# Step 1's other-half products in a pair of their own, inverse pieces ahead of the first rounds, and placings split around a key's copy: one change to a DeltaNet and PReLU feed-forward kernel

## The chip, the cores and the metric

The kernel runs on one core of one Trainium2 chip. The core has a matrix engine (TensorE, "PE" in the profile; its weight loads are "PEld"), three engines for elementwise work (VectorE "DVE", ScalarE "ACT", GpSimd "POOL"), and SyncE ("SP"), which here only issues DMA transfers. Each engine works through its own queue of instructions in order; an instruction that needs another engine's result waits on a semaphore, and everything behind it in the same queue waits with it. TensorE writes its products to PSUM (eight banks for each partition; this kernel takes them as two single banks and three pairs at the start), the other engines read them there and write to SBUF.

The metric is the device time of one execution in microseconds (us), as the median of several runs.

## The reference, cut to what matters

```python
def _attn_ref(q, k, v, beta):                      # (4, 8, 768, 48): batch, heads, sequence, head size
    k_n = k / (np.linalg.norm(k, axis=-1, keepdims=True) + 1e-06)
    state = np.zeros((B, H, D, D))
    for t in range(S):
        kt, vt, bt = k_n[:, :, t], v[:, :, t], beta[:, :, t, None]
        y[:, :, t] = np.einsum('bhd,bhde->bhe', q[:, :, t], state)
        v_old = np.einsum('bhde,bhd->bhe', state, kt)
        state = state + bt[:, :, :, None] * np.einsum('bhd,bhe->bhde', kt, vt - v_old)

def _moe_ref(x, w_in, w_out, alpha):               # x: (3072, 384), w_in: (384, 2048)
    h = x @ w_in
    g = np.maximum(h, 0.0) + alpha * np.minimum(h, 0.0)
    return g @ w_out

# the attention's y, with its heads side by side, is x of the feed-forward part
```

All of it is in 32-bit floating point. The recurrence over 768 positions is computed in chunks of 64: within a chunk a triangular system is solved, and between chunks the 48x48 state of each head is carried on.

## The kernel before, in words

A *step* n is one chunk of 64 positions of two of the four batch entries, so there are 12 chunks x 2 = 24 steps; steps 0 and 1 are the first chunk, 2 and 3 the second, and so on. For each step the kernel turns the keys on TensorE (`flip`, L430, with a ScalarE copy to `k_t`, L439 or L456), makes their products (`grams`, L502), turns the right-hand side by the inverse of a unit triangular matrix (`solve`, L884, with VectorE's `u` at L888), and makes the outputs (`outputs`, L897) and the next state (`next_state`, L916). Between these, TensorE works on the feed-forward products (L1062 and L1105, L1126 and others), which make up most of its time; they are woven between the steps' parts by an order written out by hand, which the compiler keeps on each engine.

The inverse is made for four steps at once on VectorE: 64 columns are cut in two halves of 32, and `eliminate` works through a 32x32 block by rounds of two instructions (`prod` at L594, `block` at L600). What it makes is turned back in four pieces each (`turns`, L567: `turned` and then `inverse`), and `place` and `placing` copy a step's share to where TensorE reads it: part 0 is `diag<-turned` (L764), parts 1 and 2 the two halves of `inv`, part 3 two small copies of `wgt` (L775).

For the first four steps there is a shorter way, `eliminate_small`: only blocks of 16 are inverted, and the rest is made up by three *rounds* of substitution k = 0, 1, 2 (`substitute`, L727, and the VectorE additions of `substituted`, L734 and L736). For steps 0 and 1 this is done in `first_chunk`, which runs alone, without feed-forward products to fill TensorE's gaps, since their inputs are not there yet. It begins with `off_products` (L686, L688): TensorE multiplies the turned blocks of both steps by `mid`. For heads in the upper half the product is written twice, to the own half of the partitions (`own[i]`, one PSUM pair for each step) and to the other half (`other`, one pair for both steps, one bank each). ScalarE copies the first kind to `diag` (L689), VectorE copies the second kind to `away` (L692; `aways[i]`). Then the rounds go back and forth between TensorE and VectorE, for step 0 and step 1 in turn; behind step 0's products of round 0 TensorE turns key 4, and behind those of round 1 key 5 (both into the pair that held `other`), and ScalarE copies both to `k_t` (L439). VectorE's four `inverse` pieces (`next(inverted)`) are spread between its other work: two ahead of `aways[0]`, one ahead of `aways[1]`, the last behind round 0's first addition. `place_inverse` (L741) scales the pieces to `inv` with two ScalarE instructions for each step.

Steps 2 and 3 are then done together in `second_pair`, with `alongside(products, pieces)` putting a number of feed-forward products and of weight conversions between the parts. Steps 4 and 5 are done by `attention(n)`, steps from 6 (`JOINED`) on by `burst_a`, `turn_round` and `burst_b`, and three stretches in each step take up feed-forward products and elimination rounds; `PIECES_OF` says how many elimination pieces each of a step's three stretches takes.

The tiles' dependences are tracked for a whole tile: who reads one bank of a pair waits for the last write to that pair.

Of the kernel before, what the change touches and what calls it, by code (L numbers as in the profile page):

```python
# [44 lines left out]
def kernel(  # L45
# [623 lines left out]
    def off_products(both):  # L669

        x = [act[:, FP - 4 + i].rearrange("p f i -> p (f i)") for i in both]
        x = [y.rearrange("p (h c) -> p h c", h=H) for y in x]
        for i in both:
            own = turned[0][:, i * H : i * H + H]
            nc.scalar.mul(x[i][:, :, 0:HB], own, which[:, 0:1])
            nc.vector.tensor_scalar_mul(x[i][:, :, HB:C], own, which[:, 1:2])
        n = C - LB
        own, other = [ps_big(), None], ps_big()
        own[1] = ps_big()
        for i in both:  # L680
            p = own[i][:, 0, 0 : H * n].rearrange("p (b i) -> p b i", b=H)
            q = other[:, i, 0 : G * n].rearrange("p (b i) -> p b i", b=G)
            for b in range(H):
                for t in range(2):
                    w, y = x[i][half(t), b], mid[i][half(t), b, LB:C]
                    nc.tensor.matmul(p[half(t), b], w, y)  # L686
                    if b >= G:
                        nc.tensor.matmul(q[half(1 - t), b - G], w, y)  # L688
            nc.scalar.copy(diag[i][:, :, LB:C], p)  # L689
            other_.append(q)  # L690
        return [
            lambda i=i: nc.vector.tensor_copy(out=away[i][:, :, LB:C], in_=other_[i])  # L692
            for i in both
        ]
# [43 lines left out]
    def place_inverse(n):  # L738

        for i in range(2):  # L740
            nc.scalar.mul(  # L741
                inv[n % NE][:, :, HB * i : HB * i + HB], inverse[0][:, n * H : n * H + H],
                which[:, i : i + 1],
            )

    def place(n, parts=(0, 1, 2, 3)):
        for _ in placing(n, parts):
            pass
# [709 lines left out]
    def attention(n):  # L1458

        assert n + EARLY + 1 < TURNED_K  # L1460
        copies = between_1(n + 1)
        made = through_state(n)
        now(made[:3])
        now(copies)
        now(made[3:])
        yield
        now(solve(n))
        made = grams(n + EARLY)
        now(made[:2])
        now(between_2(n + 1))  # L1470
        now(made[2:])
        scale_v(n + 1)
        yield
        now(outputs(n))
        now(next_state(n))
        load_late(n + 2)
        squares(n + EARLY + 1)
        if n == JOINED - 1:
            flips(n + EARLY + 1, n + 2)
        yield  # L1480
        if n < JOINED - 1:
            flips(n + EARLY + 1, n + 2)
        to_ffn(n)
        if n < JOINED - 1:
            place(n + 2, (0,))
        now(weigh(n + EARLY + 1))
        if n == JOINED - 1:
            load_early(TURNED_K)
        load_q(n + 3)
        load_v(n + 3)  # L1490
        yield
# [113 lines left out]
    def first_chunk(mask, inverted, convert):  # L1605

        both = (0, 1)
        ahead[0] = n_in
        aways = off_products(both)
        for i in both:  # L1610
            for _ in range(2 - i):
                next(inverted)
            aways[i]()
        now_at = {}
        for i in both:
            now_at[i] = rhs_[i]
        for k in range(3):
            for i in both:
                p = substitute(i, now_at[i], k)
                if k == 0:  # L1620
                    now_at[i] = work.tile([128, 2, G, D], FP32, name="r")
                substituted(i, now_at[i], p, k)
                if i == 0 and k < 2:
                    now(flipped(NJ + k, ps_one()))
                if (k, i) == (0, 0):
                    next(inverted)
                    assert next(inverted, None) is None
                if (k, i) == (0, 1):
                    for j in both:
                        place_inverse(j)  # L1630
                        place(j, (3,))
                    for j in (3, 2):
                        off_blocks(j, by_pool=True)
                if (k, i) == (1, 1):
                    begin_in(6)
                if i == 0 and k > 0:
                    mask(0, k - 1)
        for i in both:
            squared(NJ + i)
        for i in both:  # L1640
            rhs_[i] = now_at[i]
        weighted = solve(0)
        keys = flipped(NJ + 2, ps_one())
        now(weighted)
        for a in range(2):
            mask(1, a)
        now(keys)
        now(solve(1))
        convert(6)
        for i in both:  # L1650
            now(outputs(i))
        load_early(NJ + NKE)
        fetch_in(n_in + 4)
        for i in both:
            to_ffn(i, ps_ffn())
        norms(NJ)
        ahead[0] = FT * DM
        convert(4)
        norms(NJ + 1)
# [155 lines left out]
    n = 12  # L1815
# [15 lines left out]
    def second_pair():  # L1831

        n, m, x = 2, 3, NJ
        both = (n, m)
        now(next_state(0))
        load_late(2)
        load_v(3)
        alongside(2, 1)
        now(next_state(1))
        for _ in part(convert_on, 2):  # L1840
            pass
        load_late(3, (0,))
        fetch_in(n_in + 6)
        load_late(3, (1,))
        alongside(4, 1)
        off_product(n)
        flips(x + 3, n)
        squares(x + 2)
        now(weigh(x))
        alongside(3, 1)  # L1850
        off_product(m)
        place_inverse(n)
        place(n, (3,))
        flips(N, m)
        alongside(4, 2)
        load_q(n + 3)
        load_early(x + 1 + NKE)
        fetch_out(1)
        for i in both:
            scale_v(i)  # L1860
        now(weigh(x + 1))
        alongside(3, 1)
        y = ps_big()
        pieces, masks, now_at = [], [], {}
        for i in range(2):
            *made, last = through_state(n + i, None, y[:, :, i * G * D : (i + 1) * G * D])
            pieces += made
            masks.append(last)
        now(pieces + masks)
        place_inverse(m)  # L1870
        place(m, (3,))
        load_q(n + 2)
        load_early(x + 2 + NKE)
        now(weigh(x + 2))
        alongside(4, 2)
        for i in both:
            now_at[i] = rhs_[i]
        for k in range(3):
            y = ps_big()
            made = [  # L1880
                substitute(i, now_at[i], k, y[:, :, j * G * D : (j + 1) * G * D])
                for j, i in enumerate(both)
            ]
            for i, p in zip(both, made):
                now_at[i] = by_parity(nv[i])
                substituted(i, now_at[i], p, k)
            if k == 0:
                now(grams(x))
                squares(x + 3)
                fetch_out(2)  # L1890
                load_v(4)
                alongside(6, 4)
            elif k == 1:
                now(grams(x + 1))
                fetch_out(3)
                load_early(x + 3 + NKE)
                now(weigh(x + 3))
                alongside(6, 3)
            else:
                now(grams(x + 2))  # L1900
                alongside(5, 3)
        for i in both:
            rhs_[i] = now_at[i]
        y = ps_big()
        pieces = []
        for i in range(2):
            pieces += solve(n + i, y[:, :, i * G * D : (i + 1) * G * D])
        now(pieces)
        alongside(2, 1)
        now(grams(x + 3))  # L1910
        alongside(3, 1)
        y = ps_big()
        pieces = []
        for i in range(2):
            pieces += outputs(n + i, y[:, :, i * G * D : (i + 1) * G * D])
        now(pieces)
        alongside(4, 1, (part(blocks, PIECES), PIECES))
        for i in both:
            to_ffn(i)
        for i in both:  # L1920
            alongside(2 * (m - i), 0)
            now(next_state(i))
            load_late(i + 2)
            load_v(i + 3)
        alongside(IN_PARTS - 48, 1, (part(blocks, 1), 1))
# [78 lines left out]
    for n in range(NJ, JOINED):  # L2004
# [7 lines left out]
    assert next(late, None) is None  # L2012
    PIECES_OF = {
        JOINED: (3, WHOLE - 2 * PIECES - 6 - 2 * share - 3, 2 * PIECES),
        JOINED + 1: (0, 4, 7), JOINED + 2: (4, 5, 9), JOINED + 3: (1, 1, 4),
    }
    TURNS = [(3, 3, 4), (3, 3, 4), (4, 4, 4), (0, 5, 6)]
    FILL = {JOINED: (8, 12, 12), JOINED + 1: (10, 12, 10), JOINED + 2: (8, 10, 12)}
# [93 lines left out]
```

## Time and profile before

| | us |
|---|---|
| median of 3 runs | 635.11 (634.94 to 636.32) |
| the profiled execution | 635.72 |
| its span, first to last instruction | 634.0 |
| TensorE busy in the span | 619.7 |
| VectorE busy | 503.8 |
| ScalarE busy | 310.4 |
| GpSimd busy | 98.1 |

The span of the profiled execution is 1.7 us shorter than its time, and its time is 0.6 us above the median. All times in what follows are counted from the start of the span. In the timeline, a row gives the start, the length, the engine, the line, what it writes and reads, the shape and how many instructions of that kind were merged; in brackets at its end stands how long the engine was idle before it and what ended that. A 32-bit matmul is recorded twice, so that 16 of the program's products appear as x32. "issue" is idle time for which the profile shows nothing that was waited for.

### The profile page before, as it was taken

Reading aid. Unit: us, or ns where it says so; the run is one execution under the profiler, and the core shown is the slowest. Engines: PE = TensorE matmul, PEld = TensorE weight load, DVE = VectorE, ACT = ScalarE, POOL = GpSimd, SP = SyncE. Lnnn points to the kernel's source line nnn. Section 1 sums busy time; section 2 is a strip of 40 time slices with the busy share of each in tenths; the row PEclk is TensorE's granted clock in tenths of the full one; section 3 lists DMA queues with packets and bytes.
Section 4 is the critical chain, followed back from the end, with each engine's and each line's share of the span. In section 5 each row is a group of like instructions: output and inputs, shape, how many; then the busy total and the mean of one; then the engine's idle time right before and its main releaser. Section 6 shows DMA issues by size and latency. Waiting matters only on the chain.

```text
span 634.0 us, 21642 instructions
## 1 busy us (share of the span) xinstructions
PE 619.7 (98%) x9116; PEld 549.2 (87%) x9116; DVE 503.8 (79%) x1219; ACT 310.4 (49%) x814; POOL 98.1 (15%) x214
## 2 busy tenths in 40 slices
PE   6889999999999999999999999999999999999997
PEld 5568888567789988989989989988999999999997
DVE  5888999979989988958978968878979579486383
ACT  6878466245543245545444546335357356353230
POOL 7021211010000000000000000000053062071350
PEclk9999999999999999999999999999999999999999
DMA  7958835212253241242242121211220300100100
GB/s 122 303 126 183 251 56 170 44 38 44 46 79 54 51 76 28 45 76 36 43 77 35 37 43 27 46 32 27 46 49 12 65 15 9 32 3 1 26 1 25
DMA packets 145968, 39.26 MB, mean 62 GB/s; under 512 B 139040, under 2 KB 142256, under 8 KB 145872
## 3 DMA queue, kind: packets, MB, share of 16 engines
q1 hardware_dynamic: 144000, 37.40, 28.9%
q8 instruction: 71, 1.16, 0.7%
q10 hardware_dynamic: 1872, 0.49, 0.4%
q14 instruction: 25, 0.20, 0.1%
HBM read 33.14 MB, written 4.72 MB: 60 GB/s over the span
## 4 chain that ended last, share of the span: by engine, by line
PE 90%; ACT 3%; DVE 2%; SPq 2%; DMA 1%; issue 1%; POOL 0%; DVEq 0%; POOLq 0%; ACTq 0%
PE p_ffn L1062 17%; PE p_ffn L1126 10%; PE p_more L1396 8%; PE p_more L1126 8%; PE p_more L1062 7%; PE p_ffn L1105 7%; PE p_more L1312 5%; PE p_ffn L1302 3%; PE p_ffn L1396 3%; PE p_pair L859 3%; PE p_ffn L1307 3%; PE p_pair L790 3%; PE p_pair L502 2%; PE p_pair L897 2%; PE p_pair L884 2%; PE p_pair L841 2%
## 5 line engine op out<-in xcount | busy, mean ns | idle before, releaser
L1062 PE MATMUL p_ffn<-xt,w_in 128*128 128x256 f32 x528 | 122.8, 383 | 0.0
L1062 PEld LDWEIGHTS p_ffn<-xt,w_in 128*128 128x128 f32 x528 | 97.9, 190 | 13.4
L953 ACT COPY xt<-z 32x96 f32<-32x96 f32 x240 | 64.8, 270 | 49.7 <-DVE z L940 46.6
L1062 PE MATMUL p_more<-xt,w_in 128*128 128x256 f32 x240 | 55.7, 382 | 0.0
L1336 POOL TENSOR_TENSOR k_t<-k_t 128x128 f32<-128x128 f32 (+1 forms) x48 | 28.4, 591 | 166.6 <-ACT k_t L1331 164.1
L600 DVE TENSOR_TENSOR block<-block,prod 128x30 f32<-128x30 f32 (+9 forms) x150 | 50.0, 333 | 5.1
L802 ACT COPY inv<-p_pair 32x256 f32<-32x256 f32 x40 | 14.5, 363 | 75.1 <-DVE u L888 38.3
L1062 PEld LDWEIGHTS p_more<-xt,w_in 128*128 128x128 f32 x240 | 44.9, 190 | 6.3
L594 DVE TENSOR_TENSOR prod<-block 128x30 f32<-128x30 f32 (+9 forms) x150 | 48.6, 324 | 1.3
L419 POOL TENSOR_TENSOR beta_t<-beta_t,rec 128x8 f32<-128x8 f32 x24 | 7.0, 293 | 247.1 <-DVE rec L413 239.6
L1074 DVE SCALAR_TENSOR_TENSOR act<-act,al_t,p_ffn 128x256 f32<-128x256 f32 x72 | 31.1, 475 | 16.3 <-ACT act L1072 16.3
L1072 ACT ACTIVATE act<-p_ffn 128x512 f32<-128x512 f32 x36 | 21.5, 596 | 27.8 <-PE p_ffn L1062 27.5
L1336 POOL TENSOR_TENSOR block<-block 128x128 f32<-128x128 f32 (+1 forms) x48 | 27.7, 576 | 12.6 <-ACT block L1331 10.1
L1302 PE MATMUL p_ffn<-xt,w_in 128*128 128x256 f32 x96 | 29.3, 387 | 0.0
L1126 PE MATMUL p_ffn<-w_out,act 128*128 128x192 f32 x160 | 27.7, 327 | 0.0
L888 DVE TENSOR_TENSOR u<-p_pair,wgt 128x384 f32<-128x384 f32 x24 | 13.2, 554 | 17.6 <-PE p_pair L884 10.2
L1126 PEld LDWEIGHTS p_ffn<-w_out,act 128*128 128x128 f32 x160 | 26.3, 190 | 0.2
L1074 DVE SCALAR_TENSOR_TENSOR act<-act,al_t,p_more 128x256 f32<-128x256 f32 x40 | 17.3, 475 | 10.9 <-ACT act L1072 10.8
L869 DVE TENSOR_TENSOR r<-v_raw,p_pair 64x192 f32<-64x192 f32 (+1 forms) x66 | 23.3, 352 | 2.9 <-PE p_pair L859 1.8
L1126 PE MATMUL p_more<-w_out,act 128*128 128x192 f32 x128 | 22.3, 326 | 0.0
L1331 ACT COPY k_t<-p_more 128x512 f32<-128x512 f32 x16 | 9.4, 587 | 25.8 <-PE p_more L1312 18.9
L1396 PE MATMUL p_more<-w_out,act 128*128 128x192 f32 x128 | 21.5, 327 | 0.0
(275 smaller groups left out, 1481.2 us busy)
## 6 DMA issues: line engine op xcount, KB each, us to landing
w_out<-in_moe_w_in_dram SPq DMA_DIRECT2D x10, 512.0 KB, 5.6
v_raw<-in_v_dram SPq DMA_DIRECT2D x48, 96.0 KB, 2.8
kl<-in_k_dram SPq DMA_DIRECT2D x96, 48.0 KB, 2.4
out_dram<-o_sb SPq DMA_DIRECT2D x90, 48.0 KB, 1.7
space_out<-in_moe_w_out_dram SPq DMA_DIRECT2D x11, 384.0 KB, 4.6
ke_last<-in_k_dram SPq DMA_DIRECT2D x25, 96.0 KB, 3.2
qp<-in_q_dram SPq DMA_DIRECT2D x64, 32.0 KB, 2.2
w_out<-in_moe_w_out_dram SPq DMA_DIRECT2D x5, 384.0 KB, 5.6
```

Source lines behind the costliest of these rows:

```text
L594: nc.vector.tensor_tensor(out=prod, in0=r[:, 0:j, j : j + 1].to_broadcast([128, j, n]), in1=r[:, j : j + 1, j + 1 : HB].to_broadcast([128, ...
L600: nc.vector.tensor_tensor(out=r[:, 0:j, j + 1 : HB], in0=r[:, 0:j, j + 1 : HB], in1=prod, op=ALU.add)
L869: nc.vector.tensor_tensor(out=r[to, a], in0=v_in[to, a], in1=p[own, a, :, 0:D], op=ALU.subtract)
L953: nc.scalar.copy(to[quad(r), u, bp, t], z[quad(2 * t + u), r])
L1062: nc.tensor.matmul(p_h[:, i], w_in[:, t, (f + i) * 128 : (f + i + 1) * 128], xt[:, t], start=(t == 0), stop=(t == KT - 1),)
L1074: nc.vector.scalar_tensor_tensor(out=g[:, i], in0=g[:, i], scalar=al_t[:, f + i : f + i + 1], in1=p_h[:, i], op0=ALU.mult, op1=ALU.add,)
L1105: nc.tensor.matmul(p_o[u], gs[f // 2][:, f % 2, u * 128 : (u + 1) * 128], w_out[:, f], start=(f == 0), stop=(f == FT - 1),)
L1126: nc.tensor.matmul(p, x(i), w(i), start=(i == 0), stop=(i == FP - 1))
L1302: nc.tensor.matmul(p[:, f * 256 : f * 256 + 256], w(2, f), xt[:, 2], start=True, stop=False)
L1312: nc.tensor.matmul(q[:, j], a, b, start=True, stop=True)
L1336: nc.gpsimd.tensor_tensor(out=dst, in0=a, in1=b, op=ALU.add)
L1396: nc.tensor.matmul(p, x(i), w(i), start=(i == 0), stop=(i == FP - 1))
```

## The change

Four things are changed. In `off_products`, the other-half products of step 1 no longer go to the second bank of `other` but to the second bank of step 1's own pair. In `first_chunk`, three inverse pieces come ahead of `aways[0]` and the fourth ahead of `aways[1]`; `place_inverse(0)` comes ahead of the rounds, and with that ahead of key 4's copy on ScalarE; step 0's small copies stay behind key 4's copy, and step 1's `place_inverse` and small copies come behind key 5's copy. In `attention`, the copy `place(n + 2, (0,))` comes ahead of the turned key and query and of `to_ffn`, not behind them (this is for step 4 alone). In `second_pair` one feed-forward product moves from ahead of `through_state` to behind it, and in `PIECES_OF` two elimination rounds move from the third stretch of step 8 to that of step 9.

```diff
@@ off_products
-            q = other[:, i, 0 : G * n].rearrange("p (b i) -> p b i", b=G)
+            q = (other[:, 0] if i == 0 else own[1][:, 1])[:, 0 : G * n]
+            q = q.rearrange("p (b i) -> p b i", b=G)
@@ attention
         if n < JOINED - 1:
+            place(n + 2, (0,))
             flips(n + EARLY + 1, n + 2)
         to_ffn(n)
-        if n < JOINED - 1:
-            place(n + 2, (0,))
@@ first_chunk
         aways = off_products(both)
-        for i in both:
-            for _ in range(2 - i):
-                next(inverted)
-            aways[i]()
+        for _ in range(PIECES - 1):
+            next(inverted)
+        aways[0]()
+        next(inverted)
+        assert next(inverted, None) is None
+        aways[1]()
+        place_inverse(0)
...
                 if i == 0 and k < 2:
                     now(flipped(NJ + k, ps_one()))
-                if (k, i) == (0, 0):
-                    next(inverted)
-                    assert next(inverted, None) is None
+                if (k, i) == (1, 0):
+                    place_inverse(1)
                 if (k, i) == (0, 1):
-                    for j in both:
-                        place_inverse(j)
-                        place(j, (3,))
+                    place(0, (3,))
                     for j in (3, 2):
                         off_blocks(j, by_pool=True)
                 if (k, i) == (1, 1):
+                    place(1, (3,))
                     begin_in(6)
@@ second_pair
-        alongside(3, 1)
+        alongside(2, 1)
         y = ps_big()
...
-        alongside(4, 2)
+        alongside(5, 2)
         for i in both:
             now_at[i] = rhs_[i]
@@ PIECES_OF
-        JOINED + 1: (0, 4, 7), JOINED + 2: (4, 5, 9), JOINED + 3: (1, 1, 4),
+        JOINED + 1: (0, 4, 7), JOINED + 2: (4, 5, 7), JOINED + 3: (1, 1, 6),
```

## The prediction

> **What bounds the kernel now.** First two lines of the profile's page, then one of TensorE's idle times by releaser, then the busy times of a stretch.
>
> ```profile
> PE 619.7 (98%) x9116; PEld 549.2 (87%) x9116; DVE 503.8 (79%) x1219; ACT 310.4 (49%) x814; POOL 98.1 (15%) x214
> ...
> PE 90%; ACT 3%; DVE 2%; SPq 2%; DMA 1%; issue 1%; POOL 0%; DVEq 0%; POOLq 0%; ACTq 0%
> ```
>
> ```profile
> PE p_pair L790 <- ACT diag L764: 0.2, 1, 0.2
> ```
>
> ```profile
> 28.00:43.00 15.00, 11.60 (x442) 9.67 (x441) 11.43 (x27) 10.31 (x24) 4.81 (x8) 1.00 0.60 98
> ```
>
> TensorE is busy for 98% of the span and makes up 90% of the chain that ended last, at full clock (the 1.00). Work taken from another engine is worth something only where TensorE idles. From 28 to 43 us it idles for 15.00 - 11.60 = 3.4 us, and later for an engine only at this L790 and at L502 near 245 us (its row is below). The change touches all three and adds no arithmetic and no transfer; so the question is how much of this idle time comes back.
>
> **The first chunk.** The timeline of VectorE, of ScalarE and of TensorE:
>
> ```profile
> 28.99 1.19 DVE L567 STREAM_TRANSPOSE inverse<-block 128x256 f32<-128x256 f32 x2
> 31.54 0.36 DVE L692 COPY act<-p_pair 128x192 f32<-128x192 f32 x1 [1.36 <-PE p_pair L686]
> ...
> 36.26 0.35 DVE L734 TENSOR_TENSOR r<-v_raw,p_pair 128x192 f32<-128x192 f32 x1 [0.70 <-PE p_pair L727]
> 36.53 0.35 DVE L734 TENSOR_TENSOR r<-act,p_pair 128x192 f32<-128x192 f32 x1
> 36.80 0.55 DVE L736 TENSOR_TENSOR r<-v_raw,p_pair 128x384 f32<-128x384 f32 x1
> ```
>
> ```profile
> 30.49 0.48 ACT L689 COPY diag<-p_pair 128x384 f32<-128x384 f32 x1 [0.85 <-PE p_pair L686]
> 31.42 0.48 ACT L689 COPY diag<-p_pair 128x384 f32<-128x384 f32 x1 [0.45 <-PE p_pair L686]
> 33.43 0.59 ACT L439 COPY k_t<-p_pair 112x512 f32<-112x512 f32 x1 [1.53 <-PE p_pair L430]
> 34.01 0.91 ACT L741 ACTIVATE inv<-inverse,which 128x256 f32<-128x256 f32 x2
> ...
> 36.59 0.57 ACT L439 COPY k_t<-p_pair 112x512 f32<-112x512 f32 x1
> ```
>
> ```profile
> 32.04 0.26 PE L727 MATMUL p_pair<-act 64*64 64x48 f32 x2 [0.56 <-DVE act L692]
> ...
> 34.40 0.65 PE L430 MATMUL p_pair<-ident,ke_last 128*112 128x128 f32 x4
> 34.98 0.55 PE L727 MATMUL p_pair<-r,diag 64*64 64x48 f32 x21
> 35.79 0.39 PE L727 MATMUL p_pair<-r,diag 64*64 64x48 f32 x12 [0.26 <-issue]
> ...
> 37.21 0.26 PE L727 MATMUL p_pair<-r,diag 64*64 64x48 f32 x2 [0.52 <-ACT k_t L439]
> ...
> 39.98 0.39 PE L884 MATMUL p_pair<-r,inv 64*64 64x48 f32 x13 [0.67 <-issue]
> ```
>
> *The first wait.* Step 0's products are there when ScalarE copies them at 30.49. VectorE's copy to `away` (L692) waits until 31.54, for step 1's products too, because both lie in one pair. With step 1 in its own pair this goes. Instead VectorE first does a third inverse piece: two take 1.19, 0.6 each, so it ends about 30.75. The copy then starts at 30.75 instead of 31.54, and TensorE, which went on 0.50 after that start (32.04), goes on at 31.25: **0.79** earlier.
>
> *New waits.* Step 1's copy now shares a pair with ScalarE's copy to `diag` and waits for its end, 31.42 + 0.48 = 31.90; it ends at 32.3 (0.36, as the first). Behind it in VectorE's queue stands step 0's first addition, ready for TensorE at about 32.3 + 0.55 = 32.85. Until then TensorE has key 4's turn (0.65) and step 1's round 0 (as long) behind step 0's round 0 (0.7), to about 33.1. So the wait is hidden by 0.25; what it is later than that would count. On ScalarE `inv` of step 0 (0.91) comes ahead of key 4's copy (0.59): the fourth piece ends at 31.7, `inv` runs from 31.90 to 32.8, the copy to 33.4, and key 5's turn, which needs the pair, comes at 34.40 - 0.79 = 33.6. Hidden by 0.2.
>
> *The second wait.* Key 5's copy stands no longer behind step 1's `inv`. It follows key 5's turn at 33.6 + 0.65 = 34.3 instead of 36.59, and the 0.52 us for it at 37.21 go.
>
> **What stands in the way.** The other two idle times, 0.26 ahead of 35.79 and 0.67 ahead of 39.98, are put down to "issue": no engine is waited for.
>
> ```profile
> 35.79:39.98 4.19, 3.00 (x127) 2.56 (x127) 3.10 (x8) 4.01 (x10) 0.83 (x3) 1.00 0.52 96
> ```
>
> ```profile
> q8 instruction: 71, 1.16, 0.7%
> ```
>
> Between the two lie 127 matmuls and 127 weight loads (first two counts of the window), 254 instructions, and the page's instruction queue moved 1.16 MB in 71 packets, 16 KB for each 257 of TensorE's 2 x 9116. I read the stalls as TensorE waiting for its next block of 256 instructions. The last matmul ahead of the first begins near 35.3 (34.98 + 0.55, less 0.22, the length of one), and 128 matmuls earlier, near 31.15, an earlier block ended. From 31.15 to 35.79 is 4.64 us; from 39.1, where by the same count the next block ended, back to 35.3 and on to 39.98 is 4.68. So from the end of one block it takes some 4.66 us until the one after the next is there.
>
> Until 31.15 nothing on TensorE moves, so the block comes at 35.79 as before. TensorE gets to its end at 35.3 - 0.79 = 34.5 and idles 1.3 us: the first 0.79 are lost. Behind it the additions at 36.26, 36.53 and 36.80 come as before. Step 1's round 2 then waits for the second alone, 36.88, and goes on at 37.0 instead of 37.21; step 0's `solve` waits for the third, 37.35, and starts at 37.5, 0.2 earlier; step 1's `solve` gets to the end of the next block at 38.9 instead of 39.1. That block was asked for at 34.5, and comes at 34.5 + 4.66 = 39.2 instead of 39.98. The first chunk gains **0.79** after all, by the second refill. Bounds: 0 if the refill isn't asked for earlier; 1.05 if it is there in time (39.98 to 38.9); 2.0 if the stalls don't bind at all and all four idle times go (0.56 + 0.26 + 0.52 + 0.67). I take 0.79, the count from the block's end, on which the two rows agree within 0.04.
>
> The Trainium skill ("Runtime: NRT & Kernel Launch", section "Instruction fetch mechanics") has blocks of 256 instructions, two of which fit, and the next one is fetched while one runs, hidden behind the pace of issue. The trace agrees on the size; its 0.26 and 0.67 at the blocks' ends speak against "hidden", by which the 2.0 us would come.
>
> **The second pair.** One feed-forward product moves behind `through_state`: the same work in another place.
>
> ```profile
> L1062 PE MATMUL p_ffn<-xt,w_in 128*128 128x256 f32 x528 | 122.8, 383 | 0.0
> ```
>
> It is 122.8 / 528 = 0.23 us. I put the move at 0, with 0.23 either way as bounds: TensorE doesn't idle for an engine there now, and `through_state`, which comes earlier, gives VectorE's additions more time; if its own inputs aren't ready 0.23 earlier, the product's cover is missed.
>
> **Step 4's copy.** From the chain of waits:
>
> ```profile
> 154.85 0.38 ACT xt L967
> 155.23 0.31 ACT diag L764
> 155.54 0.04 issue
> 155.59 0.69 PE p_pair L790 x32
> ```
>
> ScalarE copies the key, the query, `xt` and then `diag`, for which TensorE idles 0.2 us. Moved ahead, `diag` is done while ScalarE waits for the key. Late next is `xt`, done at 155.24, while TensorE has L790 (0.69) first. Gain **0.23**, bounds 0 and 0.31, the copy itself.
>
> **The two elimination rounds.** Groups, then TensorE's and VectorE's timeline:
>
> ```profile
> L600 DVE TENSOR_TENSOR block<-block,prod 128x30 f32<-128x30 f32 (+9 forms) x150 | 50.0, 333 | 5.1
> ...
> L594 DVE TENSOR_TENSOR prod<-block 128x30 f32<-128x30 f32 (+9 forms) x150 | 48.6, 324 | 1.3
> ```
>
> ```profile
> 245.72 0.69 PE L502 MATMUL p_pair<-k_t 48*64 48x64 f32 x32 [0.65 <-DVE k_t L479]
> ...
> 273.23 0.56 DVE L888 TENSOR_TENSOR u<-p_pair,wgt 128x384 f32<-128x384 f32 x1 [2.48 <-PE p_pair L790]
> ```
>
> A round is 0.333 + 0.324 us, so two fewer ahead of `k_t` make it 1.3 us earlier, and TensorE waits 0.65. Gain **0.65**; bounds 0, if VectorE idles for another engine instead, and 0.65. The rounds come back in step 9; VectorE's idle 2.48 at 273.23 takes them up, and TensorE would feel only what goes beyond.
>
> **The sum.** 0.79 + 0.23 + 0.65 = 1.67. For the profiled execution 635.72 - 1.67 = 634.05; it lies 0.61 above the median of the runs shown, so for the median 635.11 - 1.67 = **633.4**.
>
> **The rivals.**
>
> (B) A block is asked for only when the one before it begins to run. Then the second refill starts at 35.79 as before, ends at 39.98, and the first chunk gains 0: 635.11 - 0.88 = 634.2. For it: two stalls can't tell a start at 35.3 from one at 35.8 well. Against it: the second would be 4.19 us then, the first 4.64.
>
> (C) The stalls don't bind (a fixed cost, or hidden once the queue has work): 2.0 + 0.88, 632.2. Against it: no idle time at 31.15, and 0.26 beside 0.67.
>
> (D) Refills get slower, being asked for while more transfers run (mean DMA share 0.52 in the window above, 0.60 from 28 to 43). At 6.0 us instead of 4.66 the next block comes at 34.5 + 6.0 = 40.5 and the one behind it at 46.5, where TensorE, which took 4.19 us for a block, was due at 39.98 + 4.19 = 44.2: 2.3 late, and the later gains make up 0.88: 636.5, slower than before. It decides from 5.5 us on (39.98 - 34.5). Nothing in the two stalls shows such a spread.
>
> (E) The gap at 245 doesn't close: 634.1.
>
> **How the numbers follow.** Forecast 46%, B 28%, C 14%, D 7%, E 5%. The range goes from 632.1, with most of C, to 634.9, with B and half a microsecond beyond, and leaves D out. From no change a measurement here can tell about 0.2%, 1.27 us, so faster is below 633.84: three quarters of the forecast, C, and a little of B and E, 0.54. Same, the rest of these: 0.36. Slower, D and what I haven't seen: 0.10.
>
> **What would show it.** Right: L692 at 30.75; key 5's copy ahead of the second `inv`; an "issue" idle time of 1.3 us up to 35.8 and `solve` going on at 39.2; no wait of L790 near 155 or of L502 near 244. Wrong: the first stall gone or much shorter (C), the second still ending at 40.0 (B), new "issue" idle times behind it (D).

## The result and the profile after

| | before | after |
|---|---|---|
| median of 13 runs each | 634.24 (633.97 to 636.32) | 633.23 (632.10 to 635.46) |
| the profiled execution | 635.72 | 632.27 |
| its span | 634.0 | 630.5 |

The ratio of the times is 0.9978, with a 95% interval from 0.9968 to 0.9987: some 1.4 us faster (0.8 to 2.0). The two medians themselves lie 1.0 apart. The forecast was 633.4 (632.1 to 634.9), a gain of 1.67. The time came as predicted, in part by luck: more runs put the kernel before 0.9 lower than the three that the forecast started from, and without that the same gain would have given 632.6. The gain itself is right within the interval, but so is the 0.88 of rival B, by which the first chunk gains nothing; the time alone doesn't decide between the two. The two profiled executions differ by 3.45, more than the medians. Why is the main subject of what follows.

The page of the profile after: busy times, and the first line of the chain of waits.

```profile
PE 619.3 (98%) x9116; PEld 549.2 (87%) x9116; DVE 502.6 (80%) x1219; ACT 309.5 (49%) x814; POOL 98.5 (16%) x214
...
PE 95%; ACT 2%; DMA 1%; issue 0%; POOL 0%; DVE 0%; ACTq 0%; DVEq 0%; POOLq 0%
```

TensorE's work is the same (619.7 before); its share of the chain grew from 90% to 95%, and VectorE's fell from 2% to 0%. From here on, line numbers in changed kernels are one higher than before (L692 is L693, L727 is L728, L884 is L885). TensorE's idle times by what ended them, those of the first chunk and behind it:

```profile
PE p_pair L687 <- ACT act L675: 0.9, 1, 0.9
...
PE p_pair L885 <- issue: 0.5, 1, 0.5
...
PE p_pair L898 <- DVE u L889: 0.4, 1, 0.4
```

Those for L692's copy, for key 5's `k_t`, for L790's `diag` and for L502's `k_t` are not in the list any more. In the timeline, first VectorE and ScalarE, then TensorE:

```profile
30.12 0.30 DVE L693 COPY act<-p_pair 128x192 f32<-128x192 f32 x1
30.36 0.65 DVE L567 STREAM_TRANSPOSE inverse<-block 128x256 f32<-128x256 f32 x1
31.39 0.36 DVE L693 COPY act<-p_pair 128x192 f32<-128x192 f32 x1 [0.39 <-ACT diag L690]
31.66 0.55 DVE L737 TENSOR_TENSOR r<-v_raw,p_pair 128x384 f32<-128x384 f32 x1
```

```profile
33.66 0.59 ACT L439 COPY k_t<-p_pair 112x512 f32<-112x512 f32 x1 [0.60 <-PE p_pair L430]
34.27 0.91 ACT L742 ACTIVATE inv<-inverse,which 128x256 f32<-128x256 f32 x2
```

```profile
33.55 0.95 PE L728 MATMUL p_pair<-r,diag 64*64 64x48 f32 x33
...
35.73 0.68 PE L885 MATMUL p_pair<-r,inv 64*64 64x48 f32 x32
36.34 0.65 PE L430 MATMUL p_pair<-ident,ke_pair 128*112 128x128 f32 x4
36.92 0.45 PE L885 MATMUL p_pair<-r,inv 64*64 64x48 f32 x16
37.85 0.45 PE L885 MATMUL p_pair<-r,inv 64*64 64x48 f32 x16 [0.48 <-issue]
```

This execution's first chunk began 0.6 earlier for a reason of its own (the first L687 runs at 28.73, L686 before at 29.29), so 0.6 is added to compare. (0.52 of it is there at 7 us already, where TensorE waited 0.5 for its first loads and not 1.0 as before.) L693 at 30.12 is then 30.7; key 5's copy at 33.66 is 34.3, ahead of the second `inv`. Where before had 0.26 of "issue" and 1.3 us were expected, TensorE runs through. One "issue" idle time is left, 0.48 in the middle of step 1's `solve`.

Later, TensorE's timeline near 153 us, and the window around 245:

```profile
151.38 1.46 PE L1106 MATMUL p_ffn<-w_out,sums 128*128 128x384 f32 x4
152.77 0.69 PE L791 MATMUL p_pair<-diag,right 32*32 32x32 f32 x32
```

```profile
240.00:250.00 10.00, 10.00 (x204) 9.26 (x203) 7.86 (x20) 7.28 (x21) 0.74 (x2) 1.00 0.23 31
```

Both engine waits are closed. Matmul for matmul, counted from the start of each span, the kernel after was 0.56 earlier at the start of the first chunk, 2.06 at before's 43 us (1.50 gained in the chunk), 2.52 at 61.5, 2.82 at 156 and 3.48 at 246.5, and that to the end. The parts: start 0.56, first chunk 1.50, near 61 us 0.46, near 155 us 0.30, near 245 us 0.66.

### The profile page after: what moved, and what is told of

It reads as the page before. It is cut to its first block, busy times and chain, and to the rows that moved or that the text cites. A ratio compares the mean times of both kernels' runs of the same rounds, so it can differ in the third digit from the quotient of the medians.

```text
span 630.5 us, 21641 instructions
## 1 busy us (share of the span) xinstructions
PE 619.3 (98%) x9116; PEld 549.2 (87%) x9116; DVE 502.6 (80%) x1219; ACT 309.5 (49%) x814; POOL 98.5 (16%) x214
## 4 chain that ended last, share of the span: by engine, by line
PE 95%; ACT 2%; DMA 1%; issue 0%; POOL 0%; DVE 0%; ACTq 0%; DVEq 0%; POOLq 0%
PE p_ffn L1063 19%; PE p_ffn L1127 10%; PE p_more L1063 8%; PE p_more L1397 8%; PE p_more L1127 8%; PE p_ffn L1106 7%; PE p_more L1313 5%; PE p_ffn L1303 3%; PE p_ffn L1397 3%; PE p_pair L860 3%; PE p_pair L791 3%; PE p_ffn L1308 3%; PE p_pair L502 2%; PE p_pair L898 2%; PE p_pair L885 2%; PE p_pair L842 2%
```

## The experiments

Two theories were tried. By the first, TensorE's "issue" idle times are its waits for the next block of instructions, and the delay of a block differs from one execution to the next, so a single profile cannot say what the first chunk gains. By the rivals, the delay is fixed, or the idle times belong to the instructions they stand at.

**The change again, unaltered.**

> The changed kernel once more, unaltered. In its profile the sum of the parts was larger than the timed gain: the last matmuls stood 3.59 us earlier from the start, 0.60 of that before the change can act (the start's own waits), 1.65 in the first chunk, 0.35 near 61 us, 0.33 near 155 us, 0.66 near 245 us. Theory 1 (TensorE's instruction blocks come after a delay that differs between executions, 3.4 and 4.0 us from a block's end there, 4.64 and 4.68 before): the later gains of 0.33 and 0.66 and both closed engine waits come again, the idle time put down to issue between 30 and 62 us differs from the 0.48 of that profile, and the median is 0.7 to 2.2 us below before. Rival (the delay is fixed and the first stall is gone for good): again no issue idle time ahead of the matmul after 128 of that stretch, 0.5 ahead of the next, and the median about 2.6 us below before (1.65 + 0.33 + 0.66).

632.87 median (632.26 to 633.7) against 634.4; ratio 0.997 (0.9958 to 0.9982), 1.1 to 2.7 us. TensorE's only "issue" idle time:

```profile
38.37 0.45 PE L885 MATMUL p_pair<-r,inv 64*64 64x48 f32 x16 [0.48 <-issue]
```

Here the first theory's guess that this idle time would differ was a miss: it was 0.48 again, as the rival had it, and the rival's 2.6 us lies just inside the interval of the time. What speaks against the rival comes from the runs below. The first chunk's start lay 0.20 earlier than in the profile of before, not 0.56; the chunk gained 1.34, the places near 155 and 245 us 0.30 and 0.59. So the start is the execution's own, and these parts came again with the change.

**Only the first chunk's part** (the hunks in `off_products` and `first_chunk`):

```diff
+            q = (other[:, 0] if i == 0 else own[1][:, 1])[:, 0 : G * n]
...
+        for _ in range(PIECES - 1):
+            next(inverted)
+        aways[0]()
```

> Only the first chunk's part of the change (step 1's other-half products in its own pair, the inverse pieces ahead of the rounds, the placings split); steps 2 to 4 and the elimination rounds as before. Both theories: L692's copy starts some 0.8 earlier, key 5's copy stands ahead of the second inv, TensorE idles near 155 (0.2 to 0.3) and near 245 us (0.65) as before. Theory 1 (the instruction blocks take part of the gain back): between 0 and 1.7 us faster, 0.8 at the median. Rival (the stalls don't bind): 1.6 to 2.0 us faster. Rival (nothing of the first chunk lasts, all of the timed gain is later): 0.0 to 0.2.

634.02 against 634.4, ratio 0.999 (0.9977 to 1.0003): 0.6 us by the ratio, and no change not excluded. In its profile:

```profile
34.71 0.39 PE L728 MATMUL p_pair<-r,diag 64*64 64x48 f32 x12 [0.52 <-issue]
38.43 0.45 PE L885 MATMUL p_pair<-r,inv 64*64 64x48 f32 x16 [0.48 <-issue]
```

```profile
240.00:250.00 10.00, 9.36 (x198) 8.45 (x197) 8.16 (x20) 5.72 (x16) 0.75 (x2) 1.00 0.28 43
```

The instructions of this chunk are those of the changed kernel, and still the idle time at the first block's end is back, with 0.52. The chunk gained 0.89 here, against 1.50 and 1.34. Near 245 us TensorE idles 0.64, as before.

**Only the later parts** (the hunks in `attention`, `second_pair` and `PIECES_OF`; the first chunk as before):

```diff
+            place(n + 2, (0,))
             flips(n + EARLY + 1, n + 2)
...
-        alongside(3, 1)
+        alongside(2, 1)
...
-        JOINED + 1: (0, 4, 7), JOINED + 2: (4, 5, 9), JOINED + 3: (1, 1, 4),
+        JOINED + 1: (0, 4, 7), JOINED + 2: (4, 5, 7), JOINED + 3: (1, 1, 6),
```

> Only the later parts (the diag copy placed ahead of the key's and the query's, the product of the second pair moved behind through_state, two elimination rounds fewer ahead of k_t); the first chunk as before. Expected by the sum: 0.2 to 0.3 at 155 us and 0.65 at 245 us, 0.9 together, no idle time for an engine at either place, and the stretch from 28 to 43 us as before (waits for L692 and key 5's copy of 0.5 each, issue idle times of 0.2 to 0.7 at the same matmuls as before, since no instruction is moved ahead of them). Rival (what is closed at 155 and 245 comes back later, VectorE being late in step 9): under 0.3 us, with a new idle time for DVE or issue behind 245 us.

633.32 against 634.4, ratio 0.998 (0.9968 to 0.9991): 1.3 us (0.6 to 2.0), for 0.88 in the sum. The first chunk, whose code is that of before, and the window around 245:

```profile
35.62 0.39 PE L727 MATMUL p_pair<-r,diag 64*64 64x48 f32 x12 [0.53 <-issue]
40.08 0.39 PE L884 MATMUL p_pair<-r,inv 64*64 64x48 f32 x13 [1.21 <-issue]
```

```profile
240.00:250.00 10.00, 10.00 (x200) 8.98 (x200) 8.28 (x20) 5.60 (x16) 0.74 (x2) 1.00 0.28 43
```

These are the same matmuls as in the profile of before, but with 0.53 and 1.21 where that had 0.26 and 0.67: the same code idled 0.8 us longer for "issue", of which 0.54 is left at 43 us. The 1.21 is above the 0.7 that was expected at most. Between 150 and 246.5 us the matmuls gained 0.95, and none of it was lost behind.

**Only the two elimination rounds.**

```diff
-        JOINED + 1: (0, 4, 7), JOINED + 2: (4, 5, 9), JOINED + 3: (1, 1, 4),
+        JOINED + 1: (0, 4, 7), JOINED + 2: (4, 5, 7), JOINED + 3: (1, 1, 6),
```

> Only the two elimination rounds moved from the stretch ahead of k_t to step 9. Expected: TensorE's wait of L502 for k_t near 245 us (0.65) gone and nothing new behind it, the wait for diag near 155 (0.2 to 0.3) as before: 0.65 earlier from 246 us to the end. Rival (the rounds are missed later): part of it comes back as an idle time behind 250 us.

One execution, 634.87 beside 634.89. The window around 245 and what is left near 155:

```profile
240.00:250.00 10.00, 10.00 (x199) 8.93 (x199) 8.69 (x21) 5.18 (x15) 0.75 (x2) 1.00 0.28 43
```

```profile
PE p_pair L897 <- issue: 0.6, 1, 0.6
...
PE p_pair L790 <- ACT diag L764: 0.2, 1, 0.2
```

As expected at 245: the wait is gone, 0.74 by the matmuls from 156 to 246.5 us, and nothing is lost from there to the end. So the 245 us part belongs to the rounds, and the 155 us part doesn't. Against the profiled execution of before, 635.72, this one is 0.85 faster. The 634.89 beside it is another execution of before, without a profile, and two single times can't show 0.7: in the series above those of before went from 633.92 to 637.26. Other differences of this execution nearly cancel: its chunk started 0.28 later than in the profile of before and gained 0.77, and behind a new "issue" idle time of 0.6 at L897, near 79 us, 0.87 is lost. The first chunk, again that of before, shows no "issue" idle time at all.

**The kernel before again.**

> The kernel before once more, unaltered, for its idle times put down to issue. Theory 1 (the block of instructions comes a varying time after it is asked for): idle times ahead of the same matmuls as in the profile of before (L727 with r,diag near 35, L884 with r,inv near 39, L727 with r,diag near 61), but of other lengths than 0.26, 0.67 and 0.22, by 0.2 or more at one of them at least, and wherever one stands, its matmul starts 1.3 to 1.5 after the end of the instruction queue's packet, as in all the profiles so far (1.29 to 1.46). Rival (a fixed delay of 4.66 from a block's end): 0.26 and 0.67 again within 0.1, since all that leads up to them is the same code.

```profile
36.24 0.39 PE L727 MATMUL p_pair<-r,diag 64*64 64x48 f32 x12 [0.54 <-issue]
40.16 0.39 PE L884 MATMUL p_pair<-r,inv 64*64 64x48 f32 x13 [0.67 <-issue]
```

The time was 635.38, beside 634.89. The idle times are 0.54 for 0.26, 0.67 again, and none near 61 us, where the first profile of before had 0.22. The rival's fixed delay fails at one of its two places; the other agreed. With the two experiments above there are four executions of before's first chunk: 0.93, 1.21, 1.74 and 0 us of "issue".

**Step 1's pair alone, and the order alone.**

```diff
-            q = other[:, i, 0 : G * n].rearrange("p (b i) -> p b i", b=G)
+            q = (other[:, 0] if i == 0 else own[1][:, 1])[:, 0 : G * n]
+            q = q.rearrange("p (b i) -> p b i", b=G)
```

> Only step 1's other-half products in its own pair; the order of pieces, placings and key 5's copy as before. If the shared pair was what the copy to away (L692) waited for, it no longer waits for the 0.4 to 0.5 between step 0's and step 1's products, but stands behind two inverse pieces only (30.2 instead of 31.54 from the start), and step 1's own copy, behind the third piece, now waits for ScalarE's diag. Key 5's copy still follows the second inv (36.6), so TensorE still idles about 0.5 for k_t near 37.2. With instruction blocks that come late (theory 1) an issue idle time stands between 34 and 36, and the gain at 43 us is 0 to 0.8 against before. Rival (the wait was ScalarE's, for the diag copies, not the pair): L692 at 31.5 as before and no gain.

VectorE, and TensorE's idle times:

```profile
30.23 0.36 DVE L693 COPY act<-p_pair 128x192 f32<-128x192 f32 x1 [0.35 <-PE p_pair L687]
...
31.58 0.36 DVE L693 COPY act<-p_pair 128x192 f32<-128x192 f32 x1 [0.40 <-ACT diag L690]
```

```profile
PE p_pair L728 <- ACT k_t L439: 1.0, 1, 1.0
```

The pair was what the copy waited for. But TensorE, 0.66 earlier, now waits 0.96 for key 5's copy, not the 0.5 that was expected: without the new order most of the gain moves into the next wait. The "issue" idle time that theory 1 expected between 34 and 36 us did not come. With none in the whole chunk, where the profile of before has 0.93, the chunk still gained 1.31, more than the 0.8 that was expected at most. The time, 633.73 beside 634.25, is a single one.

The order alone (the hunks of `first_chunk`, without that of `off_products`):

```diff
+        for _ in range(PIECES - 1):
+            next(inverted)
+        aways[0]()
...
+                if (k, i) == (1, 0):
+                    place_inverse(1)
```

> Only the order of the first chunk (three pieces, then away, the fourth, the placings split); step 1's products still in the shared pair. The copy to away still waits for step 1's products (about 31.5), so the first wait of TensorE (0.56 ahead of 32.04) stays. Key 5's copy moves ahead of the second inv, so the wait for k_t (0.52 at 37.21) goes. Theory 1: behind that the issue idle time ahead of 39.98 grows to 0.9 to 1.2 if the block comes 4.66 after the end of the one before, or is 0.7 or less if the delay varies. Rival (a fixed cost of this place): 0.67 again, and the whole 0.5 gained at 43 us.

```profile
PE p_pair L884 <- issue: 0.6, 1, 0.6
PE p_pair L727 <- DVE act L692: 0.6, 1, 0.6
```

The wait for the copy stays (0.6), that for `k_t` is gone, and "issue" did not grow to 0.9 or more, so the 4.66 of the prediction does not hold here. This idle time doesn't tell a varying delay from the rival's fixed cost, 0.67; the chunk gained 0.77, and the time is 634.33 beside 634.25. With neither edit alone do both engine waits go.

**Where the idle times stand.** The kernel before with filler matmuls ahead of the first chunk:

```diff
     for _ in range(6):
         busy(0.25, mid[1], p)
+    for _ in range(16):
+        busy(1 / 32, mid[1], p)
```

> The kernel before with 16 tiny extra matmuls in the idle time of TensorE ahead of 29 us, which count 32 instructions and write only scratch. Theory 1 (the issue idle times stand at the ends of 256-instruction blocks): both move 16 matmuls earlier in the program, to other instructions than the ones they stand at before, 128 matmuls apart as before. Rival (they belong to the instructions or the data there): the same two matmuls, L727 with r,diag after 23 and L884 with r,inv. The time within 0.5 of before.

The 16 are recorded as 32 (9148 matmuls for 9116), so the blocks' ends fall 32 recorded matmuls earlier in the program. No "issue" idle time is left between 26 and 66 us; instead TensorE waits 1.1 for `k_t`. That the idle times would come up elsewhere in the chunk was a miss, and this run settles little: the run with only the two rounds has none in the chunk either, without any shift. The time, expected within 0.5 of before, was 637.3 beside 634.25; the first chunk starts 2.42 later behind the longer filler (31.71 for 29.29). Then twice as many on the changed kernel:

```diff
     for _ in range(6):
         busy(0.25, mid[1], p)
+    for _ in range(32):
+        busy(1 / 32, mid[1], p)
```

> The changed kernel with 64 more tiny matmuls (128 instructions) in the filler ahead of the first chunk, which write only scratch: the ends of the 256-instruction blocks fall 64 matmuls earlier in the program, into the middle of step 1's round 0 (L728 with v_raw,diag), of step 1's round 2 (L728 with r,diag) and to the start of the output products (L898). The filler itself costs some 5.5 us (32 of them cost 2.6 in the kernel with 16). Theory 1: the 0.48 ahead of L885 is gone, and issue idle times stand at the new places; worked out from the changed kernel's matmul starts with 4.0 to 4.5 from a block's end to the first matmul of the block after the next, the sum of these idle times to 62 us is 2.7 to 4.2, because no long matmuls lie in these blocks. Rival (the idle times belong to the instructions they stand at, or have no limit in the queue): 0.48 ahead of the same second half of L885 and nothing else.

```profile
34.00:50.00 16.00, 15.39 (x443) 14.02 (x443) 7.89 (x20) 7.64 (x18) 4.79 (x8) 0.73 0.26 48
```

```profile
66.47 0.31 PE L842 MATMUL p_pair<-beside 48*64 48x48 f32 x3 [1.23 <-issue]
```

```profile
352.25 0.18 PE L791 MATMUL p_pair<-diag,right 32*32 32x32 f32 x1 [1.22 <-issue]
...
379.21 0.21 PE L791 MATMUL p_pair<-inv,mid 32*32 32x32 f32 x1 [1.56 <-issue]
```

The predicted 2.7 to 4.2 before 62 us did not come, and this run cannot test it: in it the granted clock was 0.73 from 34 to 50 us, and slower matmuls give the blocks more time. It does show that "issue" idle times follow the place of the blocks: 0.48 at L885 is gone, and 4.0 us (1.23 + 1.22 + 1.56) stand at three matmuls that had none in the profile after. The first of the three is the 1107th recorded matmul of the program. So is the one that waited 0.22 near 61 us in the profile of before, and 1.03 and 1.32 in the two runs of before with later loads below; but there it is a matmul of L727, and here, with 64 more ahead, one of L842. The other two are 384 recorded matmuls apart, three times 128. The time is 647.51 beside 634.89.

**Are the transfers the cause?** Three loads moved behind the early keys' load, in the changed kernel and, twice, in the kernel before:

```diff
-    load_v(2)
     for i in range(2):
         flips(N, i)
-    for i in range(2):
-        load_q(i + 2)
...
         load_early(NJ + NKE)
+        for i in both:
+            load_q(i + 2)
         fetch_in(n_in + 4)
+        load_v(2)
```

> The changed kernel with three loads of the first chunk (the third value chunk and two query chunks) issued after the early keys' load in place of ahead of it, so that less traffic stands on the DMA engines while TensorE's instruction blocks are fetched between 30 and 42 us. Theory 1a (the fetch competes with the loads): the time from a block's end to the start of its successor's fetch shrinks below 2 us, the issue idle time between 28 and 62 us goes to 0.2 or less, 0.3 to 0.6 us faster than the changed kernel. Theory 1b (the delay is the fetch's own, whatever the DMA engines do): the issue idle times stay 0.2 to 0.7 each, and the time is that of the changed kernel within 0.3, or worse where a load is now late for its first reader.

> The kernel before with the same three loads (a value chunk and two query chunks) issued after the early keys' load. Theory 1a (the fetch competes with the loads): the issue idle times of 0.26 and 0.67 shrink or go, and the fetches start less than 2 us after a block's end. Theory 1b (the delay is the fetch's own): the same idle times within 0.2 at the same matmuls.

> Once more the kernel before with three loads (a value chunk and two query chunks) issued after the early keys' load. In its first profile the instruction fetches began 1.12, 0.72 and 0.54 after the blocks' ends (2.29, 2.31 and 2.55 before), while the same edit to the changed kernel gave 1.64, 1.92 and 1.77 (1.10, 1.35 and 1.99 without it). Theory 1a (the fetch competes with the loads): 0.5 to 1.2 again. Theory 1b (the delay varies between executions, whatever the loads do): another set, between 0.5 and 3.4.

On the changed kernel, 633.6 against 634.4, ratio 0.998 (0.997 to 0.9991), no better than the change alone (0.997 in the same series). Its idle times:

```profile
34.74 0.39 PE L728 MATMUL p_pair<-r,diag 64*64 64x48 f32 x12 [0.56 <-issue]
38.20 0.45 PE L885 MATMUL p_pair<-r,inv 64*64 64x48 f32 x16 [0.21 <-issue]
59.86 0.49 PE L728 MATMUL p_pair<-r,diag 64*64 64x48 f32 x11 [0.56 <-issue]
```

On the kernel before, the first time none in the chunk and 1.03 near 61 us; the second time, of the very same kernel:

```profile
36.18 0.39 PE L727 MATMUL p_pair<-r,diag 64*64 64x48 f32 x12 [0.53 <-issue]
39.80 0.39 PE L884 MATMUL p_pair<-r,inv 64*64 64x48 f32 x13 [0.38 <-issue]
62.11 0.49 PE L727 MATMUL p_pair<-r,diag 64*64 64x48 f32 x10 [1.32 <-issue]
```

The delays from a block's end to the next fetch were 1.12, 0.72 and 0.54 the first time and 2.52, 1.88 and 2.11 the second. The times were 636.29 beside 634.25 and 636.59 beside 634.89. Then the windows from a block's last matmul to the start of the fetch, for the second block end of the second execution and the third of the first; the number before the last is the share of the DMA engines that was busy:

```profile
35.43:37.29 1.86, 1.11 (x56) 0.86 (x48) 0.88 (x4) 1.80 (x6) 1.28 (x3) 1.00 0.00 0
38.76:39.28 0.52, 0.52 (x51) 0.52 (x45) 0.52 (x3) 0.52 (x2) 0.00 (x0) 1.00 0.00 0
```

With the DMA engines idle (a share of 0.00) the fetch began 1.88 after the block's last matmul in one case and 0.54 in the other. So theory 1a, that the fetch competes with the loads, falls: the delay does not follow the transfers. What does set it stays open.

**The delays together.** The instruction queue's packet shows in the view of the transfers when the window is as long as the packet. Before, 33.42 to 34.41 us, and after, 31.55 to 32.71 (packets, MB, share of 16 engines' time), the row reads the same:

```profile
q8 instruction: 1, 0.02, 6.2%
```

6.2% is one of the 16 engines for the whole window, so the packet took about 1.0 us before and 1.15 after. In the same way, with the blocks' ends counted by matmuls in each trace, for the first three ends in the chunk (A, B, C; the idle times stand ahead of the first matmuls behind B and C; the block fetched behind A begins at B, the one fetched behind B at C; "last" is the start of a block's last matmul, "first" that of the next one):

```
kernel               fetch after last     fetch after first    TensorE's step     first L686/L687 to
                     A     B     C        A     B     C        last to first      first L1062/L1063
                                                                B     C
before               2.29  2.31  2.55     2.28  1.84  1.66      0.48  0.89        29.29 to 43.58: 14.29
before again         2.40  1.97  2.06     2.40  1.21  1.16      0.75  0.89        29.47 to 43.76: 14.29
later parts only     2.12  2.95  3.42     2.11  2.20  1.99      0.75  1.43        28.84 to 43.67: 14.83
two rounds only      2.04  1.64  2.24     2.04  1.40  2.11      0.25  0.14        29.57 to 43.09: 13.52
after                1.10  1.35  1.99     1.09  1.12  1.29      0.23  0.70        28.73 to 41.53: 12.80
after again          1.44  1.32  1.92     1.43  1.12  1.22      0.20  0.70        29.09 to 42.05: 12.96
first chunk only     1.83  2.04  2.08     1.82  1.30  1.38      0.74  0.70        28.71 to 42.11: 13.40
after, loads later   1.64  1.92  1.77     1.64  1.14  1.34      0.78  0.43        28.80 to 41.88: 13.08
```

Three readings. First, that these idle times are waits for instructions: between 30 and 42 us all profiles together have 15 idle times put down to issue, and at each the first matmul came 1.29 to 1.46 after a fetch had ended. Second, the delay ahead of the fetch varies, in the same code too: 2.04 to 2.40 at A in the four with the old first chunk, 1.10 to 1.83 in the others here, but 1.12 and 2.52 in the two executions of one kernel (the kernel before with later loads). Third, the delay goes with TensorE's own pace: over B and C of the 13 profiles without the fallen clock, the delay from the last matmul grows by 1.5 us for each 1 us of TensorE's step from last to first (correlation 0.83), and counted from the first matmul it scatters less (standard deviation 0.39 for 0.64). So a block seems to be asked for when the one before it begins to run, not when the one before that ends. If the count began exactly there, 1 us of step would add 1.0 us and not 1.5, so this is not all of it. And it is read off the traces after the fact; no experiment set it alone.

The last column is the stretch that the first chunk's part of the change can touch: 14.23 on the mean of the four executions with the old first chunk, 13.05 on that of three with the new (after, after again, first chunk only), 1.18 less. Without the "issue" times it is 13.08 to 13.52 for the old and 12.32 to 12.48 for the new: that part is steadier, within 0.44 and 0.16. (The two don't add up exactly: a shorter "issue" idle time can leave a longer wait for an engine behind it, as the 0.72 for `k_t` in the run with only the two rounds, 0.52 before.)

## Why the prediction was right, and where it was not

*The first wait, 0.79: right.* L693 at 30.12 plus 0.6 is 30.7 for 30.75, and TensorE gained 0.79 up to the first rounds (1.35 earlier at before's 32.04, of which 0.56 from the start). The two new waits were hidden as worked out: step 1's copy waited 0.39 for `diag` and TensorE never for it, and key 4's copy behind `inv` was not late either.

*The second wait: right, to the place and the time* (key 5's copy at 34.3). Run by themselves, the edit of the pair and that of the order each left one of the two waits, and the pair's alone took away the 0.56 at the one and raised the 0.52 at the other to 0.96.

*The refills: that they bind was right, their size and their start were wrong.* The failing step is "So from the end of one block it takes some 4.66 us until the one after the next is there". The two rows it was taken from, 4.64 and 4.68, agreed by chance: at the 15 idle times it was 3.8 to 5.2. And the count seems to begin where rival B had it, with the next block's first matmul. Rival B's price of 0 was wrong all the same, since the delay was not the fixed 4.19 that it took either: from first matmul to first matmul it was 3.72 to 3.73 after, after again and with the first chunk alone, and 4.46 in the later parts' run. So the idle 1.3 us up to 35.8 did not come, `solve` went on at 37.85 plus 0.6, 38.5, not 39.2, and the profiled chunk gained 1.50, not 0.79. Rival C (nothing binds, 2.0) was too high for it, since 0.48 was left. Over executions the term is 0.6 by the times of the first chunk's part alone (-0.2 to 1.5) and 1.18 by the mean profiles; 0.79 lies between, but not for the reason given. Rival D, refills that grow slower because of transfers, found no support: the longest of the 15 was 5.2, below the 5.5 from which it would decide.

What the prediction cites of the Trainium skill ("Runtime: NRT & Kernel Launch", section "Instruction fetch mechanics") needs a word too. That section says of the instruction memory in general that it is two blocks, but gives 2048 instructions, eight blocks of 256, for TensorE. The traces here go with two: at all three block ends in 13 profiles the next fetch began only behind the block's last matmul, 0.54 us at the least, and each of the 15 idle times ended 1.29 to 1.46 us behind such a fetch, which had begun after the block two before. That the fetch is hidden does not hold in this stretch, by the same 15 idle times.

*The second pair, 0: right.* Between before's 43 and 61.5 us nothing but the "issue" idle time near 61 us came or went, and that comes and goes in kernels without this edit too.

*155 us, 0.23: right in kind,* measured 0.30, near the upper bound of 0.31. *245 us, 0.65: right* (0.66; 0.74 from the two rounds alone). But what took the rounds up was not VectorE's idle 2.48, as the prediction has it. Two rows of VectorE before, then the same two after:

```profile
266.67 0.35 DVE L1150 TENSOR_TENSOR o_sb<-o_sb,p_ffn 128x192 f32<-128x192 f32 x1 [0.56 <-PE p_ffn L1126]
273.23 0.56 DVE L888 TENSOR_TENSOR u<-p_pair,wgt 128x384 f32<-128x384 f32 x1 [2.48 <-PE p_pair L790]
```

```profile
263.19 0.35 DVE L1151 TENSOR_TENSOR o_sb<-o_sb,p_ffn 128x192 f32<-128x192 f32 x1
269.75 0.56 DVE L889 TENSOR_TENSOR u<-p_pair,wgt 128x384 f32<-128x384 f32 x1 [2.48 <-PE p_pair L791]
```

The 2.48 is as long as before. The rounds made VectorE later ahead of it, and of its idle times there the 0.56 ahead of 266.67 went. TensorE felt nothing of it.

*Why the profiles differed by 3.45:* 1.50, 0.30 and 0.66 are the change, of which the first holds the luck of the refills; 0.56 is the start and 0.46 the idle time near 61 us, which another execution of before had not either. The first matmul of the chunk began anywhere from 28.71 to 29.57 us in kernels whose work up to there is the same. The median hides all this, one profile does not.

No version tried beats the change: the loads later gave nothing, and both shifts of the blocks cost more in time than a refill is worth.

## What to carry to other kernels

In a stretch of many short matmuls like this one, an "issue" idle time can differ from one execution of the same code to the next (0 to 1.74 us here): take its size from several executions, and judge an edit by what is left without it (here 13.3 to 12.4 us). A wait that is removed can show up in the next one in line until that is removed too, so edits to one chain have to be tried together as well as apart. For idle gaps that nothing else crowds, the row that ends the gap is a good price: 0.23 and 0.65 came as 0.30 and 0.66.

## What was not expected of the hardware

TensorE's blocks of instructions (71 packets of 16 KB on the page) were fetched 0.5 to 3.4 us after a block's last matmul, and this differed between two executions of one kernel by up to 1.6 us at the same block (0.54 and 2.11), with no tie found to the transfers in flight; what came after in the chunk, about 0.9 to 1.4 for the packet and 1.3 to 1.5 to the first matmul, was steady (near 61 us the latter was 1.8 twice). And 64 more tiny matmuls on the record, put into the filler ahead of the chunk, were followed by a granted clock of 0.73 for 16 us, while in all other profiles its mean over the span was 0.999 or 1.0. It is one execution, with a mean of 0.992; executions without the longer filler, of which no profile was kept, have means down to 0.994, so that the filler was the cause is not shown.
